# A written order for the first eight attention jobs, sixteen weight pieces and first chunk, with keys pooled on VectorE

## The chip, the cores and the metric

The kernel runs on one core of a Trainium2 chip. The metric is the device time of one execution in microseconds, the median of several runs. A core has five engines, each with its own instruction queue that it works off in order: TensorE (products), VectorE, ScalarE, GpSimd, and SyncE, which issues the loads. They wait for each other by semaphores.

## What is computed

An attention block, a gated layer and four weighted experts, on 2 x 576 tokens of 512 features:

```python
q_d, k_d, v_d = (a.reshape(B, H, Sd, 4, D).mean(axis=3) for a in (q, k, v))
out_up = np.repeat(sm_attn(q_d, k_d, v_d), 4, axis=2)
mask = np.abs(pos[:, None] - pos[None, :]) < 4
scores = np.where(mask, scale * q @ k.T, -1e9)
x = out_up + softmax(scores) @ v            # per head, then (1152, 512)

h = x @ w_in                                # 512 -> 2048
x = (h * sigmoid(h)) @ w_out                # 2048 -> 512

p = domain_probs / domain_probs.sum(-1, keepdims=True)
out = sum(p[:, e:e+1] * (np.maximum(x @ w1[e], 0) @ w2[e]) for e in range(4))
```

`sm_attn` is softmax attention over 144 means of four tokens; the local part sees three neighbours on either side.

## The kernel before

**Attention** is cut into sixteen jobs: per batch two blocks of 256 and 320 queries, per block four pairs of heads. Job j loads keys and queries (`kq`), values (`vw` for the windows, `vg` for the means) and goes through these steps: local scores into PSUM (S, line 369 and the mask product in 375), row maxima and subtraction on VectorE (x, 382 and 383), exponential on ScalarE (e, 387), pooling of keys and queries (the first four jobs by `pool_kq_first`, the keys by four products with an identity matrix, line 333, and a copy on ScalarE, 336; the queries on VectorE, 341; later jobs on GpSimd), scores of the means (D, 393), their maximum and exponential (n and d, 407 to 409), sums and norm (u, r, g, 390 to 420), transposes (T, 432 and 434), their evacuation by ScalarE (a, 435 to 442), the values (V, 460 and 464) with GpSimd's pooled `vd`, their sum (o on ScalarE, f on VectorE, 467 and 469) and the split of x into a rounded and a rest part (h on ScalarE, 476, l on VectorE, 477).

**The gated layer** multiplies in three passes (rounded x rounded, rounded x rest, rest x rounded), in two halves of 1024 features and four chunks of tokens each. Its weights come in pieces of 128 x 512 numbers, stored as 64-bit words that hold fp32; a piece needs two passes on ScalarE (A, 208 and 209), one on VectorE that joins them (C, 210), a rounding copy (w, 217, on ScalarE) and the rest part on GpSimd (L, 218). Pieces 0 to 7 are the first 1024 columns of w_in, 8 to 15 the rows of w_out that belong to them. For a chunk and each of eight feature tiles there is a first product over four head pairs (line 540 by `mm3`, called from `g1_step`, and for three tiles from `start_mm` as soon as each pair's x is there), then tanh on ScalarE (th, 559), the gate on VectorE (gf, 560), rounding on ScalarE (gh, 565) and rest on VectorE (gl, 566). The second product (`g2_step`) needs all eight gh and gl of the chunk.

**The experts** follow with products in line 759; the change doesn't touch them.

The order on each engine is set by a scheduler that takes instructions by a priority (`prio`, ticks) and by hand-made edges (`follow`): an edge between two instructions of one engine fixes their order without a semaphore. `FIRST_LOADS` gives the first twenty loads an order. At most some eight loads are under way; a further issue waits. A piece's buffer is one of three staging tiles or three places in `acc`, free again after C.

## Time and profile before

| | |
|---|---|
| three runs | 670.26, 672.26, 672.43 us (median 672.26) |
| profiled execution | 669.87 us |
| its span, first to last instruction | 667.6 us |
| TensorE busy | 642.5 us (96%) |
| VectorE, ScalarE, GpSimd busy | 418.4, 330.5, 245.5 us |
| granted TensorE clock, mean | 0.986 |
| loads | 44.93 MB read |

The page gives an engine's busy time, the chain that ended last and groups of instructions by line; the trace behind it answers for a stretch of time, a group by shape, or one engine's timeline. A timeline row has start, duration, engine, line, operation, output <- inputs, and in brackets the idle time before it with what ended it.

### The profile page before, as it was taken

To read this page: it belongs to the slowest core of one execution; us is meant where nothing else is said; L and a number is where in the kernel's file an instruction comes from. 1 tells how busy PE (TensorE), PEld (TensorE's weight loads), DVE (VectorE), ACT (ScalarE), POOL (GpSimd) and SP (SyncE) were. 2 spreads that over 40 slices of the span, in tenths; PEclk is the share of its full clock that TensorE was granted. 3 is DMA by queue.
4 is the path that set the end of the run, shared out by engine and by line. 5 is a ranking of instruction groups with operands and counts; after the bars stand their busy time and mean duration, and the time that the engine had idled before them with its cause. 6 is when DMAs were issued, how large, how long until landed. Compare 5 with 4: busy or idle time off the path is not lost.

```text
span 667.6 us, 13740 instructions
## 1 busy us (share of the span) xinstructions
PE 642.5 (96%) x5516; PEld 626.6 (94%) x5516; DVE 418.4 (63%) x851; ACT 330.5 (50%) x753; POOL 245.5 (37%) x346
## 2 busy tenths in 40 slices
PE   4879999999999999999999999999999999999995
PEld 4758988999999999999999999999999999999995
DVE  3569676475634644766467975568954769765444
ACT  2888765477843543454335643346533356433321
POOL 5546741114510000642356433456422654433210
PEclk9598999999999999999999999999999999999999
DMA  8975622007410400140002310012300020000001
GB/s 233 348 223 165 211 86 63 16 11 227 152 64 1 127 1 1 64 159 1 1 1 71 123 61 2 1 33 96 99 29 1 1 65 1 1 32 33 2 32 48
DMA packets 16927, 48.16 MB, mean 72 GB/s; under 512 B 2976, under 2 KB 4256, under 8 KB 16864
## 3 DMA queue, kind: packets, MB, share of 16 engines
q1 hardware_dynamic: 16864, 47.29, 22.3%
q8 instruction: 43, 0.70, 0.4%
q14 instruction: 20, 0.16, 0.1%
HBM read 44.93 MB, written 2.36 MB: 71 GB/s over the span
## 4 chain that ended last, share of the span: by engine, by line
PE 82%; DMA 6%; ACT 4%; DVE 4%; POOL 3%; issue 1%; SPq 0%; POOLq 0%; ACTq 0%; DVEq 0%
PE mm L540 52%; PE p L759 26%; DMA stg<-in_w_dram 3%; DMA vg<-in_va_dram 2%; DMA vg_f<-in_va_dram 1%; DVE gl L566 1%; DVE dec L210 1%; PE s L369 1%; ACT stg L209 1%; POOL wbuf L218 1%; PE t L432 1%; ACT dec L208 1%; PE o L464 1%; DVE acc L787 1%; POOL kq L306 1%
## 5 line engine op out<-in xcount | busy, mean ns | idle before, releaser
L540 PE MATMUL mm<-xh,wbuf 128*128 128x256 f32 (+2 forms) x1280 | 265.0, 294 | 5.4 <-DVE gf L560 3.5
L540 PEld LDWEIGHTS mm<-xh,wbuf 128*128 128x128 f32 x1280 | 208.9, 189 | 7.7 <-DVE gf L560 5.0
L540 PE MATMUL mm<-xl,wbuf 128*128 128x256 f32 (+2 forms) x640 | 187.7, 294 | 0.0
L741 POOL TENSOR_TENSOR r<-r 128x128 f32<-128x128 f32 x160 | 95.1, 607 | 177.8 <-ACT r L735 133.4
L744 DVE TENSOR_TENSOR h<-r,h 128x384 fp32r<-128x384 f32 (+1 forms) x128 | 91.8, 719 | 64.2 <-ACT h L743 64.0
L540 PEld LDWEIGHTS mm<-xl,wbuf 128*128 128x128 f32 x640 | 121.0, 189 | 0.2
L743 ACT ACTIVATE h<-r 128x384 fp32r<-128x384 f32 (+1 forms) x128 | 73.6, 578 | 93.3 <-POOL r L741 54.2
L540 PE MATMUL mm<-gh,wbuf 128*128 128x256 f32 (+2 forms) x512 | 102.6, 295 | 0.2 <-ACT acc L600 0.2
L759 PE MATMUL p<-wext,h 128*128 128x256 f32 x672 | 89.4, 276 | 0.0
L759 PE MATMUL p<-wbuf,h 128*128 128x256 f32 x672 | 82.7, 276 | 0.0
L540 PEld LDWEIGHTS mm<-gh,wbuf 128*128 128x128 f32 x512 | 81.9, 188 | 0.7 <-ACT acc L600 0.4
L759 PEld LDWEIGHTS p<-wext,h 128*128 128x128 f32 x672 | 82.4, 188 | 0.0
L759 PEld LDWEIGHTS p<-wbuf,h 128*128 128x128 f32 x672 | 79.4, 188 | 0.0
L540 PE MATMUL mm<-gl,wbuf 128*128 128x256 f32 (+2 forms) x256 | 74.0, 294 | 0.0
L741 DVE TENSOR_TENSOR r<-r 128x128 f32<-128x128 f32 x96 | 39.3, 409 | 35.6 <-ACT r L735 31.2
L735 ACT ACTIVATE r<-mm 128x512 f32<-128x512 f32 x48 | 28.6, 596 | 65.4 <-PE mm L540 65.0
L566 DVE TENSOR_TENSOR gl<-gf,gh 128x256 fp32r<-128x256 f32 (+2 forms) x64 | 39.0, 612 | 19.7 <-ACT gh L565 18.8
L540 PEld LDWEIGHTS mm<-gl,wbuf 128*128 128x128 f32 x256 | 47.8, 188 | 0.1
L218 POOL TENSOR_TENSOR wbuf<-dec,wbuf 128x512 fp32r<-128x512 f32 x24 | 32.1, 1354 | 25.9 <-ACT wbuf L217 19.8
L684 POOL TENSOR_TENSOR wext<-kst,wext 128x512 fp32r<-128x512 f32 x8 | 10.4, 1298 | 77.0 <-ACT wext L682 42.6
L560 DVE SCALAR_TENSOR_TENSOR gf<-th,mm 128x256 f32<-128x256 f32 (+2 forms) x64 | 28.4, 450 | 16.4 <-ACT th L559 15.1
L787 DVE SCALAR_TENSOR_TENSOR acc<-p,pr,acc 128x256 f32<-128x256 f32 (+1 forms) x63 | 36.1, 604 | 3.6 <-PE p L759 3.0
(138 smaller groups left out, 932.1 us busy)
## 6 DMA issues: line engine op xcount, KB each, us to landing
stg<-in_w_dram SPq DMA_DIRECT2D x25, 512.0 KB
kst<-in_w2d_dram SPq DMA_DIRECT2D x16, 512.0 KB
kst<-in_w1d_dram SPq DMA_DIRECT2D x12, 512.0 KB
acc<-in_w_dram SPq DMA_DIRECT2D x7, 512.0 KB
kq<-in_kqb_dram SPq DMA_DIRECT2D x8, 323.0 KB
kq<-in_kqa_dram SPq DMA_DIRECT2D x6, 419.0 KB
stg<-in_w1d_dram SPq DMA_DIRECT2D x4, 512.0 KB
vw<-in_vb_dram SPq DMA_DIRECT2D x8, 180.0 KB
```

What stands on the lines that cost most here:

```text
L208: first = ACT.activation(out=d, in_=v[:, :, 1].bitcast(F32), func=ACTF.Prelu, scale=2.0 ** -112, alpha=2.0 ** 32)
L218: POOL.tensor_tensor(out=l[:, c], in0=d, in1=h[:, c].bitcast(F32), op=ALU.subtract)
L540: ins = [PE.matmul(out=ps, lhsT=l, rhs=r, start=(first and i == 0), stop=(last and i == n - 1)) for i, (l, r) in enumerate(pairs)]
L560: DVE.scalar_tensor_tensor(out=gf[:, 0:n], in0=th[:, 0:n], scalar=1.0, in1=ps[:, 0:n], op0=ALU.add, op1=ALU.mult)
L566: latest[DVE] = DVE.tensor_tensor(out=gl[ft][:, 0:n], in0=gf[:, 0:n], in1=gh[ft][:, 0:n].bitcast(F32), op=ALU.subtract)
L684: b = eng.tensor_tensor(out=l[:, r], in0=x, in1=h[:, r].bitcast(F32), op=ALU.subtract)
L735: ACT.activation(out=r[:, 0:4].rearrange("p s t -> p (s t)"), in_=ps[:, 0:512], func=ACTF.Relu)
L741: latest[eng] = eng.tensor_tensor(out=r[:, o], in0=r[:, a], in1=r[:, b], op=op)
L743: ACT.activation(out=h, in_=r[:, part], func=ACTF.Copy)
L744: latest[DVE] = DVE.tensor_tensor(out=l, in0=r[:, part], in1=h.bitcast(F32), op=ALU.subtract)
L759: ins = [PE.matmul(out=ps, lhsT=x, rhs=y, start=(opens and k == 0 and i == 0), stop=(k == 3 and i == n - 1), skip_group_check=True) for i, ...
L787: DVE.scalar_tensor_tensor(out=o, in0=ps, scalar=p, in1=o, op0=ALU.mult, op1=ALU.add)
```

## The change

A name is given to each step of the first eight jobs, sixteen pieces and the first chunk (`mark`), and five lists say in which order SyncE, TensorE, ScalarE, VectorE and GpSimd run them (`written` makes an edge between neighbours). What has no name is still placed by the scheduler, between them. The keys of jobs 0 to 3 are pooled by one reduction each on VectorE instead of by products. The rounding copy w of pieces 2, 3, 7, 8, 11 and 14 runs on VectorE. ScalarE clears `qdl` as its first instruction, which brings its table load to the start. The first jobs are emitted two ticks apart instead of three.

```diff
+WHI_ON_DVE = (2, 3, 7, 8, 11, 14)
...
-    FIRST_LOADS = ("kq0", "kq1", "vg0", "vw0", "kq2", "vg1", "vw1", "kq3", "vg2", "vw2", "vg3", "vw3",
-                   "s0", "s1", "s2", "s3", "kq4", "s4", "s5", "kq5")
+    FIRST_LOADS = ("kq0", "kq1", "vw0", "s0", "vg0", "s1", "kq2", "vg1", "vg2", "vw1", "kq3", "s2", "vw2", "vg3",
+                   "s3", "s4", "vw3", "s5", "kq4", "s6", "s7", "s8", "kq5", "qt", "vw4", "s9", "s10", "kq6", "s11",
+                   "vw5", "s12", "s13", "kq7", "s14", "s15", "vw6", "vw7")
...
+    steps = {}
+
+    def mark(name, *ins):
+        steps.setdefault(name, []).extend(ins)
+        return ins[-1]
+
+    def written(names):
+        ins = [i for n in names.split() for i in steps[n]]
+        for a, i in zip(ins, ins[1:]):
+            follow(i, a, "written order")
...
-            key = (u, j) if u < 2 else u
+            mark(f"A{4 * u + j}", first, low)
+            mark(f"C{4 * u + j}", i)
+            key = u
...
-            ACT.activation(out=h[:, c], in_=d, func=ACTF.Copy)
-            POOL.tensor_tensor(out=l[:, c], in0=d, in1=h[:, c].bitcast(F32), op=ALU.subtract)
+            if 4 * u + j in WHI_ON_DVE:
+                mark(f"w{4 * u + j}", DVE.tensor_copy(out=h[:, c], in_=d))
+            else:
+                mark(f"w{4 * u + j}", ACT.activation(out=h[:, c], in_=d, func=ACTF.Copy))
+            mark(f"L{4 * u + j}", POOL.tensor_tensor(out=l[:, c], in0=d, in1=h[:, c].bitcast(F32), op=ALU.subtract))
...
-        POOL.memset(qdl, 0.0)
+        z = ac.tile([128, 1], F32, name="zero")
+        DVE.memset(z, 0.0)
+        mark("tab", ACT.activation(out=qdl.rearrange("p a b c -> p (a b c)"), in_=z.to_broadcast([128, HP * 32]), func=ACTF.Copy))
...
     def pool_kq_first(j):
-        kp = j.ps[:, 352:352 + SD]
         kd[j.b, j.hp] = a4.tile([128, SD], F32, tag="kd", name="kd")
         k4 = j.k[:, 3:3 + S].rearrange("p (n r) -> p n r", r=4)
-        for r in range(4):
-            i = PE.matmul(out=kp, lhsT=ident, rhs=k4[:, :, r], start=(r == 0), stop=(r == 3))
-            if r == 0:
-                after(i, j.group)
-        ACT.activation(out=kd[j.b, j.hp], in_=kp, func=ACTF.Copy)
+        mark(f"k{j.i}", DVE.tensor_reduce(out=kd[j.b, j.hp], in_=k4, axis=AX.X, op=ALU.add))
...
-                    t = FIRST + PER * k
+                    t = FIRST + (PER if k > 3 else 2) * k
...
+    WRITTEN = (
...
+        """tab e0 A0 e1 d0 A1 w0 w1 g0 d1 a0 e2 g1 o0 a1 A2 e3 d2 h0 A3 o1 d3 g2 A4 h1 a2 A5 w4 o2 e4 g3 w5 h2 a3
...
+        """v0 L0 v1 L1 v2 v3 L2 L3 p4 L4 L5 tp L6 p5 L7 L8 L9 L10 L11 p6 p7 L12 L13 L14 L15""",
...
-        at_tick(FIRST + PER * hp + 8, 9, start_mm, hp)
+        at_tick(FIRST + 2 * hp + 8, 9, start_mm, hp)
...
             if hf == 0 and ci == 2:
+                for names in WRITTEN:
+                    written(names)
                 close_attn()
```

On SyncE, `stg64` and `acc` loads from `in_w64_dram` are the weight pieces, `kq` keys and queries, `vg` and `vw` values. Before, from the third load on:

```order
L128 DMA vg_f0_158<-in_va_dram 72x1024
L128 DMA vw_161<-in_va_dram 72x512
L128 DMA kq_f_169<-in_kqa_dram 128x838
L128 DMA vg_f1_200<-in_va_dram 72x1024
L128 DMA vw_203<-in_va_dram 72x512
L128 DMA acc_73<-in_kqa_dram 128x838
L128 DMA vg_f2_279<-in_va_dram 72x1024
L128 DMA vw_f2_284<-in_va_dram 72x512
L128 DMA vg_f3_376<-in_va_dram 72x1024
L128 DMA vw_f3_381<-in_va_dram 72x512
L128 DMA stg64_135<-in_w64_dram 128x512
L128 DMA stg64_211<-in_w64_dram 128x512
```

and with the change, from the third load on:

```order
L130 DMA vw_161<-in_va_dram 72x512
L130 DMA stg64_137<-in_w64_dram 128x512
L130 DMA vg_f0_156<-in_va_dram 72x1024
L130 DMA stg64_231<-in_w64_dram 128x512
L130 DMA kq_f_158<-in_kqa_dram 128x838
L130 DMA vg_f1_186<-in_va_dram 72x1024
L130 DMA vg_f2_223<-in_va_dram 72x1024
L130 DMA vw_198<-in_va_dram 72x512
L130 DMA acc_73<-in_kqa_dram 128x838
L130 DMA stg64_251<-in_w64_dram 128x512
L130 DMA vw_f2_256<-in_va_dram 72x512
L130 DMA vg_f3_297<-in_va_dram 72x1024
```

The first piece moves from the thirteenth load to the fourth, and keys and values of jobs 1 to 3 come between the next pieces.

On VectorE, around the decoding of pieces 2 and 3 (`dec` is the decoded piece, `wbuf` the weights' home). Before:

```order
L210 SCALAR_TENSOR_TENSOR dec_383<-dec_383,stg64_230 128x512
L210 SCALAR_TENSOR_TENSOR dec_464<-dec_464,acc_73 128x512
L469 TENSOR_TENSOR o_234<-o_234,od_247 128x256
L477 TENSOR_TENSOR xl_72<-o_234,xh_71 128x256
L407 TENSOR_REDUCE st_265<-s_255 128x1
L408 TENSOR_SCALAR st_265<-st_265 128x1
L210 SCALAR_TENSOR_TENSOR dec_508<-dec_508,acc_73 128x512
L210 SCALAR_TENSOR_TENSOR dec_515<-dec_515,acc_73 128x512
```

and with the change:

```order
L223 SCALAR_TENSOR_TENSOR dec_420<-dec_420,stg64_251 128x512
L496 TENSOR_TENSOR xl_72<-o_258,xh_71 128x256
L409 TENSOR_REDUCE s_205<-s_205 128x4
L427 TENSOR_REDUCE st_290<-s_279 128x1
L428 TENSOR_SCALAR st_290<-st_290 128x1
L233 CAST wbuf_75<-dec_420 128x512
L223 SCALAR_TENSOR_TENSOR dec_489<-dec_489,acc_73 128x512
L435 TENSOR_SCALAR s_205<-s_205 128x5
```

Steps of jobs 0, 2 and 3 stand between, and the rounding copy of piece 2 is the CAST.

On ScalarE, at the end of the first chunk's first product: `gh6` and `gh7` are its last two rounded operands, `dec_863` and `dec_911` pieces 14 and 15, `stg64_769` and `stg64_837` pieces 16 and 17. Before:

```order
L565 ACTIVATE gh6_648<-gf_931 128x256
L209 ACTIVATE stg64_769<-stg64_769 128x512
L208 ACTIVATE dec_863<-stg64_632 128x512
L420 ACTIVATE ed_756<-ed_756,st_707 128x144
L565 ACTIVATE gh7_646<-gf_994 128x256
L208 ACTIVATE dec_911<-acc_73 128x512
L209 ACTIVATE stg64_837<-stg64_837 128x512
L420 ACTIVATE ed_904<-ed_904,st_825 128x144
L217 ACTIVATE wbuf_75<-dec_863 128x512
```

and with the change, where `dec_897` is piece 15 and `stg64_755`, `stg64_823` are pieces 16 and 17:

```order
L221 ACTIVATE dec_897<-acc_73 128x512
L222 ACTIVATE acc_73<-acc_73 128x512
L222 ACTIVATE stg64_823<-stg64_823 128x512
L486 ACTIVATE od_791<-o_776 128x80
L441 ACTIVATE ed_742<-ed_742,st_693 128x144
L235 ACTIVATE wbuf_75<-dec_897 128x512
L221 ACTIVATE dec_2124<-stg64_755 128x512
L495 ACTIVATE xh_71<-o_776 128x320
L454 ACTIVATE at_878<-t1_876 70x512
L456 ACTIVATE at_878<-t2_877 70x128
L461 ACTIVATE atd1_587<-t2_877 72x2x2x64
L587 ACTIVATE gh7_632<-gf_980 128x256
```

The pass over piece 17 now stands ahead of piece 15's rounding copy and of `gh7`; before, it stood behind `gh7`.

## Rows read from the trace of the kernel before

**Rows 1.** Stretches of time, engines' busy us, clock, DMA share and GB/s.

```profile
core 0: us, PE busy (x) PEld busy (x) DVE busy (x) ACT busy (x) POOL busy (x), PEclk, DMA share, GB/s
0.00:10.00 10.00, 3.99 (x38) 3.12 (x39) 3.28 (x8) 0.98 (x1) 5.93 (x20) 1.00 0.76 225
10.00:20.00 10.00, 6.40 (x36) 5.47 (x36) 4.42 (x16) 3.51 (x11) 4.93 (x6) 0.85 1.00 281
20.00:30.00 10.00, 9.12 (x70) 7.19 (x67) 5.19 (x9) 9.09 (x21) 4.42 (x6) 0.50 0.97 374
50.00:60.00 10.00, 9.39 (x89) 8.61 (x89) 9.38 (x19) 9.11 (x27) 6.51 (x10) 0.83 0.52 183
60.00:70.00 10.00, 9.75 (x117) 9.02 (x116) 9.44 (x26) 8.55 (x25) 5.97 (x6) 1.00 0.64 187
0.00:71.92 71.92, 55.74 (x559) 47.34 (x561) 46.98 (x118) 51.00 (x130) 38.07 (x59) 0.88 0.75 238
200.00:600.00 400.00, 399.73 (x3267) 399.41 (x3266) 263.65 (x493) 178.82 (x372) 152.92 (x209) 1.00 0.13 41
```

**Rows 2.** SyncE's and ScalarE's timelines: load issues, first piece on ScalarE.

```profile
9.84 2.58 SPq L128 DMA_DIRECT2D stg<-in_w_dram  x3
...
50.25 0.33 SPq L129 DMA_DIRECT2D acc<-in_w_dram  x1
...
19.45 0.66 ACT L208 ACTIVATE dec<-stg 128x512 f32<-128x512 f32 x1 [1.61 <-DMA stg<-in_w_dram]
```

**Rows 3.** TensorE's timeline: key products, longest stop, values, scores.

```profile
8.99 4.45 PE L333 MATMUL s<-kq,ident 128*128 128x144 f32 x16 [1.15 <-DVE s L383]
...
50.60 0.38 PE L540 MATMUL mm<-xh,wbuf 128*128 128x256 f32 x1 [2.77 <-DVE gf L560]
...
68.08 0.50 PE L460 MATMUL o<-atd,vd 72*64 72x80 f32 x8
...
68.41 0.76 PE L464 MATMUL o<-at,vw 70*64 70x64 f32 x20
...
70.54 0.71 PE L369 MATMUL s<-kq 64*64 64x70 f32 x16
```

**Rows 4.** Timelines of ScalarE and VectorE: the eighth gh and gl.

```profile
69.87 0.40 ACT L565 ACTIVATE gh<-gf 128x256 fp32r<-128x256 f32 x1
...
71.47 0.45 DVE L566 TENSOR_TENSOR gl<-gf,gh 128x256 fp32r<-128x256 f32 x1
```

**Rows 5.** ScalarE's groups by line and shape, first 71.92 us.

```profile
L217 ACT ACTIVATE wbuf<-dec 128x512 fp32r<-128x512 f32 x15 | 9.1, 630 | 0.2 <-DVE dec L210 0.2
...
L208 ACT ACTIVATE dec<-acc 128x512 f32<-128x512 f32 x7 | 4.7, 675 | 0.3 <-POOL wbuf L218 0.3
```

**Rows 6.** VectorE's groups by line and shape, first 71.92 us.

```profile
L566 DVE TENSOR_TENSOR gl<-gf,gh 128x256 fp32r<-128x256 f32 x8 | 7.3, 922 | 0.0
...
L210 DVE SCALAR_TENSOR_TENSOR dec<-dec,stg 128x512 int32<-128x512 int32 x9 | 7.2, 812 | 5.3 <-ACT stg L209 2.9 <-ACT dec L208 2.3
...
L210 DVE SCALAR_TENSOR_TENSOR dec<-dec,acc 128x512 int32<-128x512 int32 x7 | 4.8, 690 | 1.1 <-ACT dec L208 1.1
...
L390 DVE TENSOR_REDUCE s<-s 128x5 f32<-128x350 f32 x4 | 2.1, 527 | 0.0
...
L390 DVE TENSOR_REDUCE s<-s 128x4 f32<-128x280 f32 x4 | 1.8, 453 | 0.1
...
L477 DVE TENSOR_TENSOR xl<-o,xh 128x320 fp32r<-128x320 f32 x1 | 0.5, 484 | 0.0
```

**Rows 7.** Timelines of VectorE and GpSimd: two gl, and GpSimd beside the first.

```profile
53.13 2.98 DVE L566 TENSOR_TENSOR gl<-gf,gh 128x256 fp32r<-128x256 f32 x1
...
64.08 0.42 DVE L566 TENSOR_TENSOR gl<-gf,gh 128x256 fp32r<-128x256 f32 x1
...
52.30 1.04 POOL L306 TENSOR_TENSOR vg<-vg 72x512 f32<-72x512 f32 x1 [5.59 <-DMA vg<-in_va_dram]
...
53.30 1.28 POOL L218 TENSOR_TENSOR wbuf<-dec,wbuf 128x512 fp32r<-128x512 f32 x1
```

More of the change, by code (lines that the diff above doesn't have):

```diff
@@ L285, in load_vw @@
         else:
-            last_load.append(SP.dma_start(out=j.vw, in_=vb[j.b, j.hp]))
+            last_load.append(load(f"vw{j.i}", j.vw, vb[j.b, j.hp]))
     def load_vg(j):
@@ L300, in load_tail @@
         l.t = t[:, 0:64]
-        i = SP.dma_start(out=l.t, in_=qtl[l.b].rearrange('p (n r) -> p n r', r=4))
+        i = load("qt" if l.b == 0 else "qt1", l.t, qtl[l.b].rearrange('p (n r) -> p n r', r=4))
         if l.b == 0:
@@ L305, in padd @@
     def padd(o, a, b):
-        POOL.tensor_tensor(out=o, in0=a, in1=b, op=ALU.add)
+        return POOL.tensor_tensor(out=o, in0=a, in1=b, op=ALU.add)
     def pmul(o, a, b):
@@ L340, in pool_kq_first @@
             p = slice(64 * h, 64 * h + 64)
-            DVE.tensor_reduce(out=j.qd[p, h], in_=q4[p], axis=AX.X, op=ALU.add)
+            mark(f"q{j.i}", DVE.tensor_reduce(out=j.qd[p, h], in_=q4[p], axis=AX.X, op=ALU.add))
     def pool_v(j):
@@ L374, in local_scores @@
                     after(i, first[h])
+                mark(f"S{j.i}", i)
         j.group = PE.matmul(out=j.ps[:, 0:nb * WIN], lhsT=ident16, rhs=mk.rearrange("p m c -> p (m c)"),
                             start=False, stop=True, skip_group_check=True)
+        mark(f"S{j.i}", j.group)
     def local_max(j):
@@ L399, in tail_scores @@
         for hp in range(HP):
-            PE.matmul(out=l.ps[32 * hp:32 * hp + 32, 352:352 + SD], lhsT=qdl[:, hp].rearrange("p a b -> p (a b)"),
-                      rhs=kd[l.b, hp], start=True, stop=True, tile_position=(0, 32 * hp))
+            lm(l, "tD", PE.matmul(out=l.ps[32 * hp:32 * hp + 32, 352:352 + SD], lhsT=qdl[:, hp].rearrange("p a b -> p (a b)"),
+                                  rhs=kd[l.b, hp], start=True, stop=True, tile_position=(0, 32 * hp)))
         l.st = a2.tile([128, 20], F32, tag="st", name="st")
@@ L414, in norm @@
         sums = j.ps[:, 496:497 + nb]
-        DVE.tensor_scalar(out=sums, in0=sums, scalar1=1e-9, scalar2=None, op0=ALU.add)
-        DVE.reciprocal(out=j.st[:, 13:14 + nb], in_=sums)
+        mark(f"r{j.i}", DVE.tensor_scalar(out=sums, in0=sums, scalar1=1e-9, scalar2=None, op0=ALU.add),
+             DVE.reciprocal(out=j.st[:, 13:14 + nb], in_=sums))
         if nb:
@@ L419, in norm @@
             i = DVE.tensor_tensor(out=j.sm, in0=j.lo, in1=j.st[:, 13:13 + nb].unsqueeze(2).to_broadcast([128, nb, WIN]), op=ALU.mult)
-        a = ACT.activation(out=j.ed, in_=j.ed, func=ACTF.Copy, scale=j.st[:, 13 + nb:14 + nb])
-        if nb and j.i < 2:
-            behind_job.update({(0, 2 * j.i): (a, i), (0, 2 * j.i + 1): (a, i)})
+            mark(f"r{j.i}", i)
+        mark(f"g{j.i}", ACT.activation(out=j.ed, in_=j.ed, func=ACTF.Copy, scale=j.st[:, 13 + nb:14 + nb]))
     def trans(j):
@@ L459, in values @@
                 r = j.atd[:, kh, h, :] if j.c == 0 else atd[b][:, kh, 2 * hp + h, :]
-                PE.matmul(out=o[p, 320:320 + nd], lhsT=v[:, kh, p], rhs=r, start=(kh == 0), stop=(kh == 1))
+                mark(f"V{j.i}", PE.matmul(out=o[p, 320:320 + nd], lhsT=v[:, kh, p], rhs=r, start=(kh == 0), stop=(kh == 1)))
         for m in range(nb):
@@ L463, in values @@
                 p = slice(64 * h, 64 * h + 64)
[L464 to L465 removed]
+                mark(f"V{j.i}", PE.matmul(out=o[p, 64 * m:64 * m + 64], lhsT=j.vw[0:WIN, 128 * m + 64 * h:128 * m + 64 * h + 64],
+                                          rhs=j.at[:, m, p], start=True, stop=True))
         od = ac.tile([128, 80], F32, tag="od", name="od")
[L467 removed]
+        mark(f"o{j.i}", ACT.activation(out=od[:, 0:nd], in_=o[:, 320:320 + nd], func=ACTF.Copy, scale=0.25))
         j.xf = o[:, 0:320]
[L469 to L471 removed]
+        mark(f"f{j.i}", DVE.tensor_tensor(out=j.xf[:, 0:n].rearrange("p (n r) -> p n r", r=4),
+                                          in0=o[:, 0:n].rearrange("p (n r) -> p n r", r=4),
+                                          in1=od[:, 0:nd].unsqueeze(2).to_broadcast([128, nd, 4]), op=ALU.add))
     def split_x(j):
@@ L478, in split_x @@
                           op=ALU.subtract)
+        mark(f"h{j.i}", a)
+        mark(f"l{j.i}", i)
         last_x.append(i)
-        for key in {0: ((1, 0), (1, 1)), 2: ((1, 2), (1, 3)), 3: (2, 3)}.get(j.i, ()):
-            behind_job[key] = (a, i)
     plan = {}
```

112 lines of the change are left out of this document (68 added, 44 removed).

## Prediction

> **What bounds the kernel now.** I read the table of stretches first, then TensorE's timeline, then what the other engines do while TensorE waits. From 200 to 600 us TensorE is busy for 399.73 of 400 us; there is nothing to win there but by fewer products, and the change takes none of those out. In the first 71.92 us it is busy for only 55.74, and part of that at the lower granted clock: 0.50 in the stretch 20 to 30, 0.83 in 50 to 60 [rows 1]. So the time is decided by how early the first chunk's products can run without a stop; what is won there reaches the end, as the rest runs in the same order (from the end of the fourth chunk on, 189 us before, the two order lists agree on every engine).
>
> What TensorE waits for there is not one thing. Up to 19.45 us ScalarE has no weight piece: the first lands then, because SyncE queued twelve loads of keys and values ahead and issued the first piece at 9.84 [rows 2]. From there ScalarE and VectorE are the limit: ScalarE is busy for 9.09 of 10 us in 20 to 30 and 9.11 in 50 to 60, VectorE for 9.38 and 9.44 in 50 to 70 [rows 1]. TensorE's longest stop in that part, 2.77 us up to 50.60, ends with VectorE's gf [rows 3]. In the middle of it (50.25) SyncE issues the sixteenth piece, held until then by its buffer [rows 2].
>
> I measure progress by one event: the eighth gl, the last operand that the first chunk's second product needs from VectorE. It ends at 71.47 + 0.45 = 71.92; its gh on ScalarE ends at 70.27 [rows 4]. Where both kernels have then done the same work on TensorE, the difference of the two moments is the gain.
>
> **The loads.** The first piece becomes the fourth load, the second the sixth. Keys and values of jobs 1 to 3 therefore come later: two pieces of 512 KB pass in front of job 2's keys. The four pieces that unlock the first products have, with all that stands ahead of them in the new queue, 5.4 MB in front (by the list's shapes 4 x 419, 4 x 288, 3 x 144 and 4 x 512 KB). Before, 2.25 + 2.81 = 5.1 MB came in 20 us and the next 0.3 at 374 GB/s [rows 1]: about 21 us for the fourth piece, up to 22.6 if keys and values come as slowly as at first. I take 22 and its last decode step (VectorE's) at 24. Early work now waits on loads in another order, but is not slower in bytes.
>
> **Pooling keys.** Out go 16 identity products and 4 copies on ScalarE. For the first two jobs the products took 4.45 us on TensorE [rows 3]. In come 4 reductions on VectorE of 576 elements each. No row shows that shape. The floor is the 0.53 us of 350 elements, the ceiling two of them, 1.05. From 0.45 for 280 to 0.53 for 350 [rows 6] the slope is 1.1 ns an element, which gives 0.78, and I take that. TensorE's part had cover (it was waiting anyway); VectorE's has none: 4 x 0.78 = **3.1 us** on the bound engine.
>
> **Six castings of weights.** The step that rounds a decoded piece moves from ScalarE (0.63 us, [rows 5]) to VectorE for six of sixteen pieces. VectorE has no one-input copy of this kind in the trace. The upper end without contention is the two-input decode of the same 512 elements, 0.69; the lower is a two-input operation of half as many, 0.42 where it is undisturbed (a gl, [rows 7]). I take 0.69, the row of equal length: 6 x 0.69 = **4.1 us**.
>
> The Trainium skill, page VectorE: DVE Perf Modes, section on the perf-mode tier table, lists a copy of fp32 within SBUF at twice the rate of a two-input operation; by that the six would cost about 0.42 each, an estimate, and the sum would be 1.6 us smaller. No run here shows it yet.
>
> **What VectorE and GpSimd do to each other.** A gl that starts at 53.13 takes 2.98 us while GpSimd runs a piece's low part from 53.30 for 1.28 and another right behind [rows 7]; another, undisturbed, takes 0.42. Over the first 71.92 us the eight gl average 0.92 us and the nine decodes from the staging buffers 0.81 against 0.69 of the seven others [rows 6]: excess 8 x 0.50 + 9 x 0.12 = 5.1 us over 24 operations, 0.21 each. GpSimd was busy for 38.07 of the 71.92 us [rows 1]; after the change about the same work of GpSimd has to fit into less time, so I take 0.24 each, and 30 operations instead of 24 if the castings suffer too: 7.2 us, **2.0 more** than before. The bounds: no more than before (0), and every one of the 30 hit as the gl were, 0.50 each (+10).
>
> The Trainium skill, page SBUF — State Buffer, section SBUF: two separate sides, says that a two-port VectorE operation, or one with two SBUF inputs, and a GpSimd operation exclude each other for a whole instruction. The rows on the gl agree; the page adds that copies count too, and so speaks against moving them off ScalarE.
>
> **The sum for VectorE up to the eighth gl.** Busy before: 46.98 us [rows 1]. By the two order lists, one local sum and its norm (0.53 for the sum, the like for the scaling, two short ones: some 1.4 us) now come later, and two decodes (2 x 0.69) and one job's f and l (0.48 for the l, the like for the f) earlier. 46.98 - 1.4 + 1.4 + 1.0 + 3.1 (keys) + 4.1 (castings) + 2.0 (blocking) = 57.2 us. It starts with the first keys; these land at 4 us as before. Up to the fourth piece at 24 us its list holds 41 instructions, by the same durations some 17 us, so 3 us are idle: 4 + 57.2 + 3 = 64.2. Waits on other engines: 6% as in 50 to 70, of the 40 us left: 2. The eighth gl ends near **66**.
>
> **The sum for ScalarE.** Up to 71.92 us before: 51.00 [rows 1]; it was busy without a break from the gh on, so up to the gh 51.00 - 1.65 = 49.35. Its list loses 4 copies, 4 castings (two of the six were behind that gh anyway) and one exponential, and gains three passes of decoding at 0.67 and five evacuations of 0.2 to 0.6: no difference beyond 0.5 us. About 12 us lie before the fourth piece is decoded at 23, so 37 us follow: gh at 60 without any wait. GpSimd's 38.07 us [rows 1] lose some and gain none; it isn't the bound. So VectorE is, by 5 us.
>
> TensorE at that moment: one job's values (0.50 and 0.76 overlapping, 1.0 us) [rows 3] are done that weren't before; one and a half jobs' scores (0.71 each without the mask's product, some 1.0 with it, [rows 3]) and five products (0.12 apart, as 3267 in 400 us, [rows 1]) aren't: 1.0 us behind. The last group can start only when the gl has ended, and in the strict order no product of the next tile fills in: 0.45. **Gain: 71.92 - 66 - 0.45 - 1.0 = 4.5 us.** A stop like the one at 50.60 was followed by the stretch with clock 0.83; I expect the like once more and no difference from it, with 1.7 us (0.17 of 10) as the bound to either side.
>
> The profiled execution took 669.87 us: 669.87 - 4.5 = 665.4, and I say **665**. The median of the three runs shown, 672.26, is 2.4 us above that execution, which the range has to take in.
>
> **Rivals.**
> - *ScalarE is the bound* (0.24). The castings cost 0.42, blocking doesn't grow and waits are filled by the other jobs' steps. Then gh ends at 60, gl at 60.5: 71.92 - 60.5 - 0.45 - 1.0 = 10 us, **660**. For it: ScalarE's idle time before falls mostly ahead of 19.45. Against: VectorE's list is full.
> - *The shared port* (0.15), slower. VectorE blocks at 0.50 for each of 30 operations, as the eight gl did: 30 x (0.50 - 0.24) = 7.8 us more, the eighth gl at 74, **673 to 674**. It decides above 0.39 each, where nothing is won. This is the exclusion on the page named above, at the price of the rows here.
> - *Late pieces in ScalarE's order* (0.12). A pass over piece 17 now stands in front of the casting of piece 15 and the eighth gh; before, it came behind that gh. 16.6 MB lie in the queue up to it. At 281 to 374 GB/s it lands at 46 to 61 us, before it is asked for; at 238, the mean of the first 71.92 us [rows 1], at 70, and with 4 us of ScalarE behind it the eighth gl ends at 74, a loss of 3. The queue will hardly be as slack as before; at a rate between, 250, it lands at 66, the eighth gl ends at 70, **about 670**, nothing won.
>
> **How the numbers follow.** The likeliest (0.49) is VectorE as the bound: 665, its own range 661 to 669. With the rivals, 657 to 674 leaves out no more than 2 in 10: below it is ScalarE's case with 2 to 3 us of later waits gone too, above it the port at its full price. What can be told from no change is 0.3%, 2 us. Faster by more: nearly all of the likeliest and of the first rival, 0.70; within: most of the late pieces and the likeliest's edge, 0.13; slower: the port and a rest, 0.17.
>
> **What would show it.** Right: the eighth gl near 66, VectorE over 90% busy from 24 us on, castings of 0.42 to 0.69 with some far longer, the first decode on ScalarE near 9 us instead of 19.45, TensorE waiting before the last group of the first second-product tile. Wrong: an eighth gl under 62 (then the bound was ScalarE) or over 70 (then the port or the loads, told apart by VectorE's mean times and by a ScalarE wait on a load), or a change behind 100 us.

## The result and the profile after

The change made the kernel slower: median 674.07 us against 670.34, ratio **1.0057** [1.0038, 1.0075], some 3.8 us. Some executions are about 2% longer than the rest, whatever the kernel; the medians include them, the ratios leave them out. The profiled execution took 674.38 us, its span is 672.5; that is 4.5 and 4.9 us more than before.

In the changed kernel products stand in line 561 (540 before), gf and gl in 582 and 588, gh in 587, decoding in 221 to 223, the rounding copy in 235 (ScalarE) and 233 (VectorE), the evacuation of a second product in 622 (600 before). Stretches of time, columns as in [rows 1]:

```profile
20.00:30.00 10.00, 7.80 (x77) 6.18 (x77) 7.96 (x24) 7.17 (x19) 4.62 (x4) 0.83 0.99 351
50.00:60.00 10.00, 8.68 (x107) 7.82 (x106) 9.38 (x23) 10.00 (x28) 7.54 (x10) 1.00 0.57 192
60.00:70.00 10.00, 6.15 (x57) 4.89 (x57) 8.26 (x16) 6.68 (x18) 4.84 (x4) 0.68 0.45 133
70.00:80.00 10.00, 10.00 (x99) 8.61 (x98) 3.92 (x10) 5.13 (x15) 6.01 (x12) 0.81 0.43 137
0.00:66.88 66.88, 46.67 (x496) 38.08 (x498) 51.96 (x129) 51.00 (x129) 40.77 (x58) 0.95 0.82 262
24.00:66.88 42.88, 34.04 (x386) 28.80 (x388) 36.56 (x91) 39.81 (x104) 27.16 (x31) 0.92 0.76 251
150.00:160.00 10.00, 8.18 (x70) 7.78 (x69) 5.63 (x9) 6.97 (x15) 3.18 (x4) 1.00 0.60 188
200.00:600.00 400.00, 399.73 (x3256) 399.31 (x3256) 263.33 (x494) 179.94 (x375) 150.78 (x206) 1.00 0.13 40
```

Up to 60 us things went as meant. From 60 to 70 TensorE ran 57 matrix instructions where the kernel before ran 117 [rows 1], the clock granted was 0.68, and in 150 to 160 there is a second gap: 8.18 busy; the same stretch before has 9.81:

```profile
150.00:160.00 10.00, 9.81 (x84) 9.62 (x83) 5.48 (x7) 8.14 (x17) 6.35 (x5) 1.00 0.69 218
```

The first gap, on TensorE's timeline of the changed kernel (start, duration; in brackets the idle time before, and what ended it):

```profile
62.20 0.36 PE L561 MATMUL mm<-gh,wbuf 128*128 128x256 f32 x1
64.69 0.58 PE L561 MATMUL mm<-gl,wbuf 128*128 128x256 f32 x1 [2.12 <-DVE gl L588]
65.07 0.42 PE L561 MATMUL mm<-gh,wbuf 128*128 128x256 f32 x1
66.63 0.81 PE L479 MATMUL o<-atd,vd 72*64 72x80 f32 x8 [1.14 <-ACT dec L221]
67.19 1.32 PE L483 MATMUL o<-at,vw 70*64 70x64 f32 x20
...
69.37 1.20 PE L385 MATMUL s<-kq 64*64 64x70 f32 x16
```

VectorE's timeline in the same stretch:

```profile
63.39 1.24 DVE L588 TENSOR_TENSOR gl<-gf,gh 128x256 fp32r<-128x256 f32 x1
64.56 1.52 DVE L223 SCALAR_TENSOR_TENSOR dec<-dec,stg 128x512 int32<-128x512 int32 x1
66.00 0.48 DVE L496 TENSOR_TENSOR xl<-o,xh 128x320 fp32r<-128x320 f32 x1
66.40 0.48 DVE L588 TENSOR_TENSOR gl<-gf,gh 128x256 fp32r<-128x256 f32 x1
```

And the eighth gh on ScalarE's:

```profile
64.67 0.42 ACT L587 ACTIVATE gh<-gf 128x256 fp32r<-128x256 f32 x1
```

The seventh group waits 2.12 us for its gl; then job 6's values wait 1.14 us. The row names a decoding pass on ScalarE, but the tile `o` has one buffer, and it comes free with job 5's l (66.00 to 66.48), which stands behind the joining step of piece 16 (64.56). The eighth gl ends at 66.88. Behind the stop everything is long: 1.32 us for values that took 0.76, 1.20 for scores that took 0.71 [rows 3]. The granted clock is 0.50 from 63.5 to 73.7, and from 66.6 on TensorE is busy throughout:

```profile
66.60:73.70 7.10, 7.07 (x62) 6.25 (x62) 3.83 (x10) 1.92 (x5) 2.89 (x6) 0.50 0.66 210
```

The second gap, first ScalarE's timeline of the changed kernel, then the row of TensorE's that waits for it:

```profile
158.01 0.66 ACT L222 ACTIVATE stg<-stg 128x512 int32<-128x512 uint16 x1 [1.63 <-DMA stg<-in_w_dram]
158.58 0.64 ACT L221 ACTIVATE dec<-stg 128x512 f32<-128x512 f32 x1
159.13 0.62 ACT L235 ACTIVATE u<-dec 128x512 fp32r<-128x512 f32 x1
159.65 0.64 ACT L622 ACTIVATE acc<-mm 128x256 f32<-128x256 f32 x2
```

```profile
160.06 0.39 PE L561 MATMUL mm<-gh,wbuf 128*128 128x256 f32 x1 [1.84 <-ACT acc L622]
```

TensorE needs a bank that ScalarE evacuates; ScalarE's list has a pass on a later piece in front, which waits 1.63 us for its load.

**Where the time went.** I added up what TensorE's matrix instructions up to a moment take at full clock without a gap (0.1133 us for 256 columns, 0.1455 for 320, 0.1735 for 384, the others by undisturbed rows); the rest of the time is lost. Both kernels have the same matrix instructions but for those of the key products: 32 records for the 16 products of the prediction, all before 31 us. I count them at 0.128 us, 4.1 in all (they came every 0.257, so half of their time is in "lost"); they are no lead for the kernel before, so the lead of the changed one is the difference of the two rows and 4.1.

| lost up to | 60 us | 80 | 140 | 180 | 300 |
|---|---|---|---|---|---|
| before | 29.8 | 31.5 | 34.3 | 37.1 | 39.0 |
| changed | 27.0 | 36.5 | 39.8 | 45.4 | 48.3 |
| lead of the changed kernel | 6.9 | -0.9 | -1.4 | -4.2 | -5.2 |

So a lead of 6.9 us at 60 us is gone 20 us later, and 2.8 us more are lost between 140 and 180, where the change was not meant to touch anything.

### The profile page after: what moved, and what is told of

It is laid out like the page before. It is cut to its first block, busy times and chain, and to the rows that moved or that the text cites. A ratio compares the mean times of both kernels' runs of the same rounds, so it can differ in the third digit from the quotient of the medians.

```text
span 672.5 us, 13690 instructions
## 1 busy us (share of the span) xinstructions
PE 640.6 (95%) x5484; PEld 623.1 (93%) x5484; DVE 422.5 (63%) x862; ACT 327.8 (49%) x744; POOL 246.9 (37%) x345
## 4 chain that ended last, share of the span: by engine, by line
PE 85%; DMA 5%; ACT 4%; DVE 3%; POOL 1%; issue 1%; SPq 0%; ACTq 0%; POOLq 0%; DVEq 0%
PE mm L561 53%; PE p L781 26%; DMA stg<-in_w_dram 3%; DMA vg<-in_va_dram 2%; PE s L385 2%; PE t L451 1%; PE o L483 1%; ACT dec L221 1%; ACT stg L222 1%; PE o L479 1%; DVE dec L223 1%; PE s L412 1%; DVE acc L809 1%; PE s L392 0%; PE t L453 0%
## 5 line engine op out<-in xcount | busy, mean ns | idle before, releaser
L561 PE MATMUL mm<-gh,wbuf 128*128 128x256 f32 (+2 forms) x512 | 106.1, 299 | 2.3 <-ACT acc L622 1.8
L561 PEld LDWEIGHTS mm<-gh,wbuf 128*128 128x128 f32 x512 | 84.1, 191 | 3.2 <-ACT acc L622 2.0
L561 PE MATMUL mm<-gl,wbuf 128*128 128x256 f32 (+2 forms) x256 | 75.5, 298 | 2.5 <-DVE gl L588 2.4
L588 DVE TENSOR_TENSOR gl<-gf,gh 128x256 fp32r<-128x256 f32 (+2 forms) x64 | 36.4, 574 | 20.4 <-ACT gh L587 20.4
L236 POOL TENSOR_TENSOR wbuf<-dec,wbuf 128x512 fp32r<-128x512 f32 x24 | 32.7, 1370 | 31.5 <-ACT wbuf L235 12.4
```

Of the source, the lines that this page charges most:

```text
L236: mark(f"L{4 * u + j}", POOL.tensor_tensor(out=l[:, c], in0=d, in1=h[:, c].bitcast(F32), op=ALU.subtract))
L561: ins = [PE.matmul(out=ps, lhsT=l, rhs=r, start=(first and i == 0), stop=(last and i == n - 1)) for i, (l, r) in enumerate(pairs)]
L588: latest[DVE] = mark(f"gl{c}_{ft}", DVE.tensor_tensor(out=gl[ft][:, 0:n], in0=gf[:, 0:n], in1=gh[ft][:, 0:n].bitcast(F32), op=ALU.subtract))
```

## The experiments

Every run is compared with the kernel before on its own chip. "Lost" is counted as above in each run's profiled execution, which can lie off the median: that of the run without TensorE's order took 675.43 us and that with more repeats 674.62, 3.2 and 5.3 above. "Late" says whether ScalarE's order from 145 to 190 us was written as before. Where products are repeated, the repeats (3.1 us, 4.4 in the run with more of them) count as work, so the useful loss is that much larger.

| run | median us, ratio to before [95%] | lost 60 to 80 | lost 140 to 180 | late |
|---|---|---|---|---|
| before / changed (profiled) | 1.0057 [1.0038, 1.0075] | 1.7 / 9.5 | 2.8 / 5.6 | |
| late pieces behind | 672.84, 1.0035 [1.0016, 1.0053] | 7.0 | 5.7 | |
| next tile's groups fill in | 673.73, 1.0054 [1.0034, 1.0074] | 9.8 | 5.3 | |
| evacuations first | 674.00, 1.0046 [1.0022, 1.0071] | 10.1 | 6.3 | |
| no order on TensorE | 672.24, 1.0019 [0.9990, 1.0049] | 5.3 | 5.4 | |
| late order as before | 673.09, 1.0029 [1.0007, 1.0051] | 9.4 | 3.2 | yes |
| before with changed late order | 675.73, 1.0090 [1.0062, 1.0118] | 1.8 | 7.6 | |
| repeated products | 668.78, 0.9970 [0.9946, 0.9994] | 5.0 | 2.8 | by itself nearly |
| copies back on ScalarE | 671.86, 1.0022 [0.9996, 1.0047] | 8.4 | 4.8 | |
| repeats + late | 669.43, 0.9994 [0.9966, 1.0022] | 5.0 | 3.1 | yes |
| before + keys on VectorE + late | 674.45, 1.0051 [1.0025, 1.0078] | 5.2 | 3.0 | yes |
| repeats + late + copies back | 672.79, 1.0042 [1.0015, 1.0068] | 5.6 | 3.3 | yes |
| more repeats + late | 669.32, 0.9991 [0.9963, 1.0019] | 4.0 | 5.2 | yes |
| repeats + late + keys on TensorE | 681.93, 1.0165 [1.0130, 1.0200] | 6.1 | 4.0 | yes |
| **repeats + late + pieces behind** | **667.54, 0.9966 [0.9944, 0.9987]** | 3.3 | 3.7 | yes |
| the last two together | 684.01, 1.0208 [1.0173, 1.0242] | 4.8 | 2.0 | yes |
| repeats + late + pieces behind + jobs 0, 1 first | 671.50, 1.0003 [0.9984, 1.0022] | 6.0 | 4.8 | yes |
| late + jobs 0, 1 first | 671.50, 1.0015 [1.0000, 1.0030] | 9.0 | 3.7 | yes |

**Four first runs: where is the loss?** Pieces 16 and 17 behind the eighth gh and gl:

```diff
+            if 4 * u + j in (16, 17):
+                for a in (first, low):
+                    follow(a, steps["gh0_7"][0], "late pieces")
+                follow(i, steps["gl0_7"][0], "late pieces")
```

> Decoding of pieces 16 and 17 (two passes each on ScalarE, one joining step each on VectorE) is put behind the eighth gh and gl; all else as in the changed kernel. There the values of job 6 start at 66.63, right after the l of job 5 (66.00 to 66.48), which stands behind the joining step of piece 16 (64.56, 1.52 us). Theory A (late pieces on VectorE and ScalarE hold up the sixth job's values): they start near 64.7, the eighth gl ends near 65 instead of 66.88, the stretch at half clock (63.8 to 72.9) shrinks or goes; 2 us gained without, up to 5 with the clock, so a ratio to the kernel before of 0.998 to 1.003 instead of 1.0057. Theory B (TensorE's written order leaves it nothing to do in the wait): the stop from 62.4 on stays, the clock falls as before, under 1.5 us gained, 1.0035 to 1.0057. Theory C (the loss lies behind 100 us, ScalarE's passes waiting for loads): nothing gained, or 1 us lost as these pieces' buffers come free later.

TensorE's list, with the second tile's groups between those of the first (H0_1_3 is the fourth group of the second tile of the first chunk's second product, T6 and V6 are transposes and values of job 6):

```diff
-  H0_0_2 H0_0_3 H0_0_4 H0_0_5 T6 H0_0_6 V6 H0_0_7 H0_1_0 H0_1_1 H0_1_2 T7 H0_1_3 ... H0_1_7 V7
+  H0_0_2 H0_0_3 H0_0_4 H0_1_0 H0_1_1 H0_0_5 T6 H0_1_2 H0_1_3 H0_1_4 H0_1_5 H0_0_6 H0_1_6 V6 H0_0_7 T7 H0_1_7 V7
```

> Only TensorE's list is changed: the groups of the second tile of the second product stand between the groups of the first, ahead of job 6's values (two in front of the sixth group, four in front of the seventh, one in front of the values), and the transposes of job 7 come after the first tile. Theory B (TensorE has nothing to do in the wait of 62.4 to 66.6): seven groups of 0.34 us, 2.4 us of work, fill it, the clock stays at 1.00 in 64 to 73 and 2.4 to 5 us are gained: 0.998 to 1.002 of the kernel before. Theory A (the late pieces on VectorE set the end): the groups fill the wait, but values and eighth gl stay where they are; with the clock still at half, 1 to 2 us: 1.003 to 1.004. Theory C: 1.0057, since the loss lies behind 100 us.

Passes of pieces 22 and 23 behind the evacuations (`follow(a, steps[f"ya2_{4 * u + j - 22}"][0], ...)` in the same place):

> The two ScalarE passes of pieces 22 and 23 are put behind the first and second evacuation of the third chunk's second product, all else as in the changed kernel, where TensorE stands still for 1.84 us up to 160.06 for these evacuations, which stand behind a pass that waits 1.63 us for its load. Theory C (ScalarE's order is the cause of that stop): it goes, 1.8 us gained, ratio 1.0030 instead of 1.0057. Rival D (the loads come too late anyway): the stop returns in the fourth chunk, where its first products need these pieces' results or its tanh waits behind them, and the ratio stays between 1.0045 and 1.0065.

TensorE's list and `H0_0_7 S8` taken out of `WRITTEN`:

> TensorE's whole written list is dropped (the scheduler places its products by priority, as in the kernel before); loads, castings, key pooling and the other engines' lists stay. Theory B (TensorE's strict order is the cause): most of the loss goes, 0.997 to 1.001 of the kernel before. Theories A and C: TensorE's order is not what it waits for, the ratio stays at 1.004 to 1.008, with another stop in 60 to 75 while the other engines' times stay within 1 us (eighth gl near 67).

None settles it alone. With the late pieces behind, some 1.5 us come back (0.22%, and the intervals overlap). Filling the wait with the next tile's groups brings nothing: the clock stays at 1.00 up to 74 us, but then TensorE has nothing left and stops for 3.15 us, and the half clock comes there instead (TensorE's timeline of that run, then its stretches there):

```profile
76.77 0.81 PE L479 MATMUL o<-atd,vd 72*64 72x80 f32 x8 [3.15 <-ACT atd L461]
```

```profile
70.00:80.00 10.00, 6.24 (x66) 4.67 (x62) 3.53 (x9) 4.06 (x12) 5.92 (x12) 0.73 0.61 185
80.00:90.00 10.00, 10.00 (x77) 9.73 (x78) 4.46 (x14) 3.77 (x13) 3.10 (x5) 0.76 0.28 88
```

With two evacuations in front, the stop at 160 shrinks to 0.72 us and one of 1.97 appears at 169.70, before the fourth chunk's products. The run without TensorE's list upsets my yardstick: its eighth gl ends at 79.13, twelve us after the changed kernel's and seven after the kernel before's [rows 4], in an execution that took 675.43 us, only 1.0 more than the changed kernel's 674.38. By its median the run is faster than the changed kernel, but the intervals overlap, and no trace shows where the gl ends in a median execution:

```profile
78.33 0.80 DVE L588 TENSOR_TENSOR gl<-gf,gh 128x256 fp32r<-128x256 f32 x1
```

**The late order.** ScalarE's order of the third and fourth chunk, named pass by pass (F and B the two passes of a piece):

```diff
+  gh2_5 F18 gh2_6 th2_7 F19 w18 gh2_7 w19 F20 B21 F21 w20 B22 ya2_0 ya2_1 w21 F22 B23 ya2_2 w22 F23 B24 ya2_3
+  ...
+  gh3_7 w29 B31 F30 F31 w30 ya3_0 w31 ya3_1 ya3_2 ya3_3
```

> The changed kernel, with ScalarE's order of the third and fourth chunk (from the sixth gh of the third chunk to the last evacuation of the fourth, decode passes of pieces 18 to 31 among them) written as the kernel before has it; nothing ahead of 140 us differs. Theory C (about 2.8 us of the loss are ScalarE's late order, a by-product of the rescheduling: from 140 to 180 us TensorE's products fall behind full rate by 5.65 us, and by 2.8 in the kernel before): that falls to about 3, ratio 1.001 to 1.003 instead of 1.0057. Rival D (the loads of these pieces set the pace, whatever the order): it stays at 5 to 6 us in other places, ratio 1.0045 to 1.0065. Theories A and B (the loss is made at 60 to 75 us): the same as D.

In the kernel before, the same place with the changed kernel's list (`... w20 gh2_7 w21 B23 F22 B24 F23 w22 ya2_0 ya2_1 ...`):

> The mirror image: the kernel before, with ScalarE's order of the third and fourth chunk as the changed kernel has it, and nothing else of the change. Theory C: slower by about 2.8 us, ratio 1.003 to 1.005, with TensorE waiting for the third chunk's first evacuation near 156 us. Rival D: no difference, 0.999 to 1.001. By either, the first 130 us are as before.

Both runs speak for the order. In the changed kernel the gap in 150 to 160 is gone (compare 8.18 above) and the ratio falls by 0.28%, 1.9 us, though the intervals overlap:

```profile
150.00:160.00 10.00, 10.00 (x91) 10.00 (x90) 6.28 (x10) 8.19 (x18) 4.66 (x4) 1.00 0.52 170
```

In the kernel before it costs 0.9%, clear of noise, but twice what I expected and in another place, so it shows that the list matters and not what it costs in the changed kernel. The stop ends with a gf, since the last job ends 3.5 us later there than in the changed kernel and the passes now stand in front of the third chunk's tanh:

```profile
150.49 0.39 PE L555 MATMUL mm<-xh,wbuf 128*128 128x256 f32 x1 [4.31 <-DVE gf L576]
```

Over the runs with ScalarE's late list written as before (ten), 140 to 180 us lose 2.0 to 5.2, 3.6 on average; over the six of the changed kind without it 4.8 to 6.3, 5.5 on average. The list alone isn't all of it, then, but the 1.9 us agree.

**The stop and the clock.** TensorE gets work that needs nothing new:

```diff
+        if main_at[1] == 0 and db == 1:
+            for r in range(9):
+                mark(f"K{r}", *mm3(ps[:, 0:n], [...first group of this tile...], True, True))
-  H0_0_4 H0_0_5 T6 H0_0_6 V6 H0_0_7
+  H0_0_4 H0_0_5 T6 K0 K1 K2 K3 K4 K5 H0_0_6 K6 K7 K8 V6 H0_0_7
```

> The changed kernel with 27 products more on TensorE in front of the two stops, six groups of three ahead of the seventh group of the second product's first tile and three ahead of job 6's values: they repeat the first group of the second tile into that tile's own bank, which the real group then overwrites; 3.06 us at full clock in 3.26 us of waiting. Theory E (half of the lead is lost because the clock falls to half behind the stop, 63.8 to 72.9 us, just where TensorE has all its operands): the clock stays at 1.00 there, 2.5 to 3.5 us gained, ratio 1.0005 to 1.002. If the clock costs nothing, because TensorE waits for the same events anyway: no gain, 1.005 to 1.007. If it falls at the next stop instead (job 7's values near 77 us): 1.003 to 1.006 and the half-clock stretch some ten us later.

0.9970, 5.8 us better than the changed kernel, more than any theory gave. Part is the late order: the scheduler, given other times, put the evacuations of the third chunk nearly where the kernel before has them, and 140 to 180 us lose 2.8 instead of 5.6. Of the rest, some 3 us, the stretch from 60 to 80 gives 1.4: it lost 9.5, and now 5.0 and the repeats' 3.1. By the same count about 1.5 more come back between 80 and 140 us, where this run's order differs too. The stretches from 60 to 80:

```profile
60.00:70.00 10.00, 8.50 (x82) 7.88 (x81) 8.05 (x17) 6.58 (x17) 5.13 (x4) 0.88 0.49 145
70.00:80.00 10.00, 8.99 (x114) 8.12 (x114) 3.94 (x9) 5.04 (x14) 6.02 (x13) 1.00 0.52 149
```

TensorE runs 196 instructions in these 20 us, 27 of them repeats, instead of 156, with VectorE and ScalarE no busier; the clock is 0.88 and 1.00 instead of 0.68 and 0.81. To take the late order out of it, both together:

> The two edits that gave the most, together: the 27 repeated products ahead of the stops, and ScalarE's order of the third and fourth chunk written as the kernel before has it. The scheduler had by itself put the evacuations back to nearly that order in the run with the products alone (0.997). If late order and clock are the two parts of the loss: against the run with the late order alone (1.0029) the products are worth 2 to 3 us, ratio 0.9985 or less, and against the products alone nothing is added: 0.995 to 0.999. If the products gain by something else (another order between 75 and 140 us), the ratio comes out above 1.000.

Against the late order alone 0.35%, 2.3 us, within the 2 to 3 expected, but the intervals overlap, and 0.9994 missed both bounds that I gave (0.9985 and 0.999). Against the changed kernel's 1.0057 [1.0038, 1.0075] the two edits together are clear of noise: they undo the loss. With repeats at more places:

> As the run with the repeated products and the late order, with the products where that run's trace still has stops: four groups ahead of job 6's transposes (1.50 us there), two behind, three ahead of job 6's values, and four ahead of job 7's values (1.00 us). TensorE runs without a stop from 58 to 80 us. If stops cost only by the clock behind them, which stayed at 1.00 there: no difference, 0.995 to 0.999, or 0.5 us lost where the last four groups take longer than the wait. If the clock still falls between 75 and 85 us without them: 1 to 2 us faster.

No difference by the median, and in its profile (of a slower execution, see above) the clock is 1.00 in every stretch of 60 to 80 us: the rest of the loss there is no longer the clock.

**The parts of the change.** The copies back on ScalarE (`WHI_ON_DVE = ()`), in the changed kernel and then with stop and late order mended:

> The changed kernel with the six rounding copies back on ScalarE (six of 0.63 us, placed by the scheduler), all else as in the changed kernel. By the prediction's own sums VectorE, the bound, gets 3.3 us back (the copies took 0.55 us on average) and ScalarE, at 10.00 of 10 us in 50 to 60, gets 3.8 more. If VectorE is the bound up to the eighth gl: that ends at 64 to 65 instead of 66.9, ratio 1.002 to 1.005. If ScalarE is: at 68 to 70, ratio 1.007 to 1.010. Theories C and E (the loss is made behind the eighth gl): the ratio moves by less than 2 us either way, 1.004 to 1.008.

> As the run with the repeated products and the late order, and the six rounding copies back on ScalarE. With clock and late order out of the way the eighth gl decides again: if VectorE is the bound there, 2 to 3 us faster than with the copies on VectorE, 0.993 to 0.996; if ScalarE is (10.00 of 10 us busy in 50 to 60), 2 to 4 us slower, 1.000 to 1.004; if both are equally late, no difference, 0.996 to 0.999.

The first came out 2.4 us better than the changed kernel (the intervals overlap), its eighth gl 2.8 us *later* (69.71), behind a wait for ScalarE's gh. None of its three expectations fits, and again the yardstick is no guide:

```profile
69.01 0.70 DVE L588 TENSOR_TENSOR gl<-gf,gh 128x256 fp32r<-128x256 f32 x1 [1.32 <-ACT gh L587]
```

The second, 1.0042 against 0.9994 (the intervals overlap a little), speaks for some 3 us from moving the copies to VectorE, with ScalarE the tighter engine. It is not shown apart from their place: on ScalarE the scheduler places them, on VectorE the list does. The keys, alone in the kernel before:

> The kernel before with one part of the change: the keys of the first four jobs pooled by one reduction each on VectorE, instead of 16 products and four copies; ScalarE's late order is written as in the kernel before, so that rescheduling doesn't blur it. By the prediction's sum, which put 4 x 0.78 us on VectorE's path to the eighth gl: 3 us slower, 1.003 to 1.005. If they lie in VectorE's idle time ahead of the first weight piece at 19.45 us: between 0.997 and 1.001, with the eighth gl within 1 us of 71.9.

1.0051: 3.4 us, close to the 3.1 that the prediction booked, in part by luck, for the eighth gl moved by 4.7 us, to 76.62 from 71.92. And the reverse, keys on TensorE within the written order:

> As the run with the repeated products and the late order (0.9994), and the keys of jobs 0 to 3 pooled on TensorE again (16 products and four copies, each behind its job's local scores in the written order). VectorE's list gets 3.0 us shorter, all of it ahead of 20 us. If these reductions lie on the path to the eighth gl even in the written order, as they do without one (1.0051): 2 to 3 us faster, 0.994 to 0.997, eighth gl at 64 to 65. If VectorE waits there for loads and TensorE anyway: no difference, 0.998 to 1.001.

Both expectations were wrong: 1.0165, 11 us lost. TensorE's timeline shows why. The key products write into the bank in which VectorE still subtracts the maxima from the scores, so they wait for it, and the next job's scores wait behind them:

```profile
6.74 2.40 PE L354 MATMUL s<-kq,ident 128*128 128x144 f32 x8 [1.03 <-DVE s L409]
9.07 1.20 PE L393 MATMUL s<-kq 64*64 64x70 f32 x16
10.20 0.41 PE L400 MATMUL s<-mask,ident 128*128 128x280 bf16 x1
11.65 2.40 PE L354 MATMUL s<-kq,ident 128*128 128x144 f32 x8 [1.03 <-DVE s L409]
```

There are four such waits (1.03 to 1.12 us) and four groups of 2.3 to 2.4 us; the kernel before waits once for two jobs (1.15, [rows 3]). The first product with a weight, in this run and then in the one with repeats and late order:

```profile
35.72 0.58 PE L569 MATMUL mm<-xh,wbuf 128*128 128x256 f32 x1
26.37 0.58 PE L563 MATMUL mm<-xh,wbuf 128*128 128x256 f32 x1
```

So the same reduction is a loss in the kernel before and a gain in this written order; another place for the key products was not tried.

**A version that beats both.** Late pieces behind, repeats and late order:

> As the run with the repeated products and the late order (0.9994), and decoding of pieces 16 and 17 put behind the eighth gh and gl. If their steps hold up the values of job 6 and the eighth gl: the l of job 5 and that gl end 1.5 us earlier, 0.996 to 0.998. If TensorE's work up to 80 us waits for other things (the steps of jobs 6 and 7 on ScalarE): no difference, 0.998 to 1.001.

0.9966 [0.9944, 0.9987]: faster than the kernel before by some 2.3 us and than the changed one by some 6. Job 5's l ends at 66.66, not 1.5 us earlier as expected (66.37 in the run without this edit), but the seventh gl starts 1.1 us later in this execution (64.99 against 63.86), and the values of job 6 follow without a stop; 60 to 80 us lose 3.3 instead of 5.0. The profiled execution as a whole took 669.30 us, the other run's 667.57, so the traces don't show the gain that the medians give. The interval overlaps those of the runs beside it; that it is the best of them is likely, not shown. With the keys on TensorE as well (1.0208, where I expected 0.992 to 0.995) the loss of those repeats:

> Both edits of the two runs beside it. If each gains by itself, 3 to 4.5 us together: 0.992 to 0.995 of the kernel before, the fastest here. If both work on the same wait, no more than the better of the two.

**The first 40 us.** Executions of one and the same written order differ early: job 3's l ends between 38.2 and 43.0 us. In the changed kernel the first piece was there after 0.19 us of waiting; in the run with more repeats, ScalarE waits 1.47 us for it, and job 1's exponential stands behind:

```profile
10.27 0.66 ACT L221 ACTIVATE dec<-stg 128x512 f32<-128x512 f32 x1 [1.47 <-DMA stg<-in_w_dram]
10.83 0.64 ACT L222 ACTIVATE stg<-stg 128x512 int32<-128x512 uint16 x1
11.37 0.39 ACT L408 ACTIVATE s<-s 128x280 f32<-128x280 f32 x1
```

```diff
-  tab e0 A0 e1 d0 A1 w0 w1 g0 d1 a0 ...        n0 u0 C0 C1 r0 n1 k2 ...
+  tab e0 e1 d0 g0 d1 A0 A1 w0 w1 a0 ...        n0 u0 r0 n1 C0 C1 k2 ...
```

> As the fastest run so far (0.9966: repeated products, late order, pieces 16 and 17 behind), and the steps of jobs 0 and 1 (second exponential, exponentials and norms of the means on ScalarE; norm and maximum of the means on VectorE) put ahead of the decoding of the first two pieces, in whose loads' wait they stood: 0.2 to 1.5 us per load from one execution to the next, and TensorE's scores of job 2 start at 13.97 to 16.33. If that wait sets the first 40 us: scores of job 2 near 12 us in every execution, 1 to 3 us gained, 0.992 to 0.995. If the weight pieces are what the first products wait for: no difference or 1 us lost, 0.996 to 0.999.

> The changed kernel with the late order (1.0029), and the same edit to the first two jobs; no repeated products, pieces 16 and 17 as in the changed kernel. If the wait for the first two pieces sets the first 40 us: 1.000 or less. If an earlier start only lengthens the stop at 62 to 66 us and the half clock behind it: 1.002 to 1.004.

Job 2's scores start at 12.10 and 11.80 instead of 13.97, but the time does not follow: job 1's evacuated transposes now stand behind the two pieces (a stop of 2.1 us at 17 us), and in the first run 2.55 us are lost before job 7's values. The best run became 0.4% slower by it (the intervals just overlap), outside both expectations; the other (1.0015, between its two expectations) moved by less than its interval.

## Why the prediction was wrong

- **The yardstick failed.** "I measure progress by one event: the eighth gl." It was forecast for 66 and ended at 66.88, 5.0 us earlier than before; the time still went the other way. The sum took TensorE as 1.0 us behind at that moment; by the count above it was about 2, so some 3 us of the lead were left. By 80 us that was a loss of 0.9: the step that failed is the one from the event to the end. With the copies back on ScalarE the gl came 2.8 us later, in an execution 2.6 us shorter. The event says when the first tile of the second product can end; it doesn't say how much other work TensorE has done or has ready. The kernel before had filled its wait with other tiles and jobs; the changed one came to the event with 57 instructions in ten us behind it.
- **"I expect the like once more and no difference from it"**, the clock, with 1.7 us as the bound. The row of the kernel before was a stretch where TensorE waited for operands anyway. Here the stop (62.4 to 66.6, with two products in it) came just ahead of a stretch with all operands there: from 66.6 to 73.7 TensorE is busy throughout at 1.2 GHz, which takes 3.5 us from it, twice the bound. With the stop filled 2.3 to 3 us came back, 1.4 of them from 60 to 80 us.
- **"What is won there reaches the end"**, since order lists agree from 189 us on. They differ up to there, and I didn't read what stands between 100 and 189. The scheduler, given new times, put ScalarE's evacuations behind passes that wait for loads: 1.9 us by the run that undid it (2.8 by the count of lost time). The prediction named "a change behind 100 us" as what would prove it wrong, and it did.
- **The sum for VectorE was right by cancellation.** Busy up to the eighth gl 51.96 us, not 57.2; idle 14.9, not 9. Of the 5.2 us too much, 1.6 are the copies' and 3.6 the blocking's, as the rows show. The terms, in VectorE's groups up to then:

```profile
L223 DVE SCALAR_TENSOR_TENSOR dec<-dec,stg 128x512 int32<-128x512 int32 x10 | 8.1, 807 | 2.8 <-DMA kq<-in_kqb_dram 1.8 <-ACT stg L222 0.7 <-DMA acc<-in_w_dram 0.4
L223 DVE SCALAR_TENSOR_TENSOR dec<-dec,acc 128x512 int32<-128x512 int32 x7 | 5.4, 773 | 1.8 <-DMA vg<-in_va_dram 1.1 <-issue 0.7
L588 DVE TENSOR_TENSOR gl<-gf,gh 128x256 fp32r<-128x256 f32 x8 | 4.4, 554 | 0.0
L233 DVE CAST wbuf<-dec 128x512 fp32r<-128x512 f32 x6 | 3.2, 547 | 0.0
L350 DVE TENSOR_REDUCE kd<-kq 128x144 f32<-128x576 f32 x2 | 1.5, 754 | 3.5 <-DMA kq<-in_kqa_dram 3.5
```

  A reduction of keys took 0.75 (forecast 0.78). A copy took 0.42 undisturbed where the sum had 0.69. The estimate of 0.42 that the prediction worked out from the Trainium skill's page VectorE: DVE Perf Modes, section on the perf-mode tier table, was right. Blocking was 0.12 us an operation (8 gl by 0.13, 17 decodings by 0.10, 6 copies by 0.13 over their undisturbed times), half of the 0.24 taken and a quarter of the rival's 0.50: gl that had averaged 922 ns [rows 6] came down to 554, because fewer of them met a low part. Copies suffer too: one took 1.18 us at 49.43, beside GpSimd's piece of 1.33 from 49.00. With this row the trace agrees with the Trainium skill's page SBUF — State Buffer, section SBUF: two separate sides, on copies too:

  ```profile
  49.43 1.18 DVE L233 CAST wbuf<-dec 128x512 fp32r<-128x512 f32 x1
  49.00 1.33 POOL L236 TENSOR_TENSOR wbuf<-dec,wbuf 128x512 fp32r<-128x512 f32 x1 [1.88 <-ACT wbuf L235]
  ```

- **VectorE was not the bound alone.** "VectorE over 90% busy from 24 us on": 36.56 of 42.88, 85%; ScalarE 39.81, 93%. Its gh, put at 60 "without any wait", came at 64.67. The first decode was early as forecast (8.12), the fourth piece's joining step later (26.08 to 26.77 instead of 24).
- **The rivals.** The shared port did not decide. The late pieces did hold up the end, not by late loads (nothing waits for them up to 69 us) but by their place: one joining step and three passes in front of job 5's l and the eighth gh and gl. Putting them behind brought 1.5 us in the changed kernel and 1.9 with the other two edits, each time with intervals that overlap.

What stays open: whether the repeated products help by the clock alone, since they also change the order from 75 to 140 us; what the load order, the clearing of `qdl` on ScalarE and the two ticks are worth, which were not run alone; and why the runs with the late list written still lose between 2.0 and 5.2 us from 140 to 180.
